# First four layer-norm tiles in one chain, last four normalised later, last output chunks in even shares

## The chip, the core and the metric

The kernel runs on one core of a Trainium2 chip. The metric is the device time of one execution in microseconds (us); the time before is the median of three executions. A profile shows one execution: what each engine does (TensorE, written PE, with its weight loads PEld; VectorE, DVE; ScalarE, ACT; GpSimd, POOL; SyncE, SP, which here only issues DMAs), when, and what ended the idle time before it. "L612" is line 612 of the kernel before.

## The reference

A transformer block's two branches over the same layer norm, x being 2048 tokens of 512 features:

```python
x = A_x
xn = _layernorm(x, axis=-1)
s = _A_ref(xn, A_wqkv, A_wo)                               # softmax attention, 32 heads of 16
g = _silu(_B_ref(xn, B_w_gate, B_w_up, B_w_down))          # ((xn Wg) * (xn Wu)) Wd, 1792 wide
return x + s * g
```

In `_A_ref`, `scores = einsum("bhqd,bhkd->bhqk", q, k) * scale`, then softmax, then the product with v, then `@ wo`. All is float32.

## The kernel before

Tokens are cut into 16 tiles of 128 and 4 chunks of 512. Matmuls read a float32 number as two parts, a rounded high part and the low rest, and make three products (high by high, high by low, low by high) for one. So each operand is *split*: a copy that rounds (`hi`), and a subtraction (`lo`).

**The start** (`early`, from L705). x is loaded tile by tile into `raw_x` (the buffer `ks` in the profile) and V, after the first four tiles the first weights of k, q (`w1r`, `w0r`) and of v. The layer norm of a tile is `ln_stats` (L204, L205, VectorE), the root `ln_root` (L208, ScalarE), five small operations `ln_scale` (L214 to L220) and `ln_apply` (L234 on VectorE for odd tiles below 8, L235 on ScalarE for the others). `ln_turn` (L246) transposes the tile on TensorE into a PSUM bank `xT`; for chunk 0 ScalarE copies it as the high part (L254) into `fh`, and `ln_low` (L259, VectorE) makes the low part `fl`. For the other chunks ScalarE copies it twice (L250, L251) and GpSimd subtracts. Tiles 0 and 1 go through that as a first chain, tiles 2 and 3 as a second, with matmuls of zeros (`warm`, L730) before and between them. `split_raw` splits the first weights on GpSimd; its first operation is made to wait for the last `ln_apply` of the four.

Then TensorE runs through 253 products (L267) of k, q and v, counted by `n`. A table `at` says which layer-norm step of tiles 4 to 15 is issued ahead of which product: for each chunk the products at which its four tiles' statistics, applications and transpositions stand. Every engine works in the order in which the program issues (a manual schedule; SP's order alone is the scheduler's). Some of the products make scores ahead (L610), whose row maxima VectorE takes (L612). q and k go through DRAM on the way to the scores (`KD`, `QD`).

**The main part.** 256 steps of the outer loop; in each, about 8 exponentials (`expo`: TensorE L632, ScalarE L634), 16 products pv with V (`block`, L645), and as many other products as a `Filler` gives: projections, the feed-forward branch, at last the output projection (`ending`). pv's result is added to a running sum: copied by ScalarE and added by GpSimd (L656, L63), and in the last rounds added by VectorE straight from PSUM (L653).

**The end.** `ending` goes through the output chunks in pairs of tiles: chunks 0 and 1 in two pairs each, the first pair of chunk 3, two pairs of chunk 2, the second pair of chunk 3. How many rounds a pair is spread over is an iterator in the outer loop:

```python
if fil.done:
    parts = iter([3, 2, 3, 2, 2, 2, 1, 2])
    fil = Filler(ending(), lambda n: next(parts))
```

For each chunk the finished heads, written to `OD` in DRAM by `finish`, are read back and split by `o_split` through `split_rows` (GpSimd). When a pair's product is done, `end` multiplies it on VectorE by the gate (L477), and `add` adds x on GpSimd and stores the result. The last heads are divided and transposed by `last_heads` (L692 to L697), after which the last products (L554) and multiplications follow.

Of the kernel before, what the change touches and what calls it, by code (L numbers as in the profile page):

```python
# [14 lines left out]
OP = mybir.AluOpType  # L15
# [6 lines left out]
NT = S // P  # L22
NC = S // 512
ND = D // P
# [7 lines left out]
LEAD = 86  # L32
# [16 lines left out]
def body(ctx, tc, x, wqkv, wo, wg, wu, wd, out):  # L49
    nc = tc.nc  # L50
# [72 lines left out]
    def soon(n, fn):  # L123

        if n:
            waiting.append((steps[0] + n, fn))
            waiting.sort(key=lambda w: w[0])
        else:
            fn()
# [45 lines left out]

    def split_raw(name, raw, after=None):
        hi, lo = [wtile(name + n) for n in "hl"]
        cast = pool.tensor_copy(hi, raw)
        if after is not None:
            tc.add_manual_dep(cast.ins, after.ins.name, BEHIND, reason="keeps the port free for the layer norm")  # L180
        pool.tensor_tensor(lo, raw, hi, op=OP.subtract)
        return hi, lo

    norm = {}
# [8 lines left out]
    def ln_open(tts):  # L193
        n = len(tts)
        g = [qp.tile([P, n, 2], F32, name=f"mv{n}", bufs=2)] + [qp.tile([P, n], F32, name=f"{v}{n}", bufs=2)
                                                              for v in ("r0", "e1", "mr")]
        for t, tt in enumerate(tts):
            norm[tt] = g, t
        norm[tts] = g
# [7 lines left out]
    def ln_root(tts):  # L207
        nc.scalar.activation(norm[tts][1], norm[tts][0][:, :, 1], AF.Sqrt, bias=eps)  # L208
# [25 lines left out]
            return nc.vector.tensor_scalar(xt, xt, e[:, t:t + 1], mr[:, t:t + 1], op0=OP.mult, op1=OP.add)  # L234
        return nc.scalar.activation(xt, xt, AF.Identity, bias=mr[:, t:t + 1], scale=e[:, t:t + 1])  # L235

    def split_rows(raw, hi, lo):
        pool.tensor_copy(hi, raw)
        pool.tensor_tensor(lo, raw, hi, op=OP.subtract)

    def ln_turn(tt):
        c, t = divmod(tt, 4)
        xt = tokens(tt)
        norm["x", tt] = pt = psum("x" if c else "s", f"xT{tt}")
        for d in range(ND):
            nc.tensor.transpose(pt[:, d * P:(d + 1) * P], xt[:, d * P:(d + 1) * P], ident)  # L246
        hi, lo = [x[c][:, :, t * P:(t + 1) * P] for x in (xh, xl)]
        if c:
            raw = norm["raws"][t]
            nc.scalar.activation(raw, pt, AF.Copy)  # L250
            nc.scalar.activation(hi, pt.rearrange("p (d q) -> p d q", d=ND), AF.Copy)  # L251
            pool.tensor_tensor(lo, raw.rearrange("p (d q) -> p d q", d=ND), hi, op=OP.subtract)
        else:
            nc.scalar.activation(hi, pt.rearrange("p (d q) -> p d q", d=ND), AF.Copy)  # L254

# [183 lines left out]
    def o_split(c, tiles):  # L439

        for d, (oh, ol) in enumerate(tiles):
            heads = 8 if c < NC - 1 or d < ND - 1 else 4
            n = heads * DH
            raw = (wtile(("w1r", "w0r")[d]).rearrange("p d q -> p (d q)") if d < 2 else
                   fst["fp"].tile([P, D], F32, name="wdr", bufs=2))
            dma(raw[:n], OD[c][8 * d:8 * d + heads, 0:DH])
            soon(4 + 5 * d // 2, lambda raw=raw[:n], oh=oh[:n], ol=ol[:n]: split_rows(raw, oh, ol))
        ops[c] = now[0], tiles

    def small_tiles():  # L450
# [31 lines left out]
        dma(out[tt * P:(tt + 1) * P], yt)  # L482

    def add(tt, yt, xt):
        pool.tensor_tensor(yt, yt, xt, op=OP.add)
        dma(out[tt * P:(tt + 1) * P], yt)

    def o_terms(c, t):
# [148 lines left out]
    def block(todo):  # L637

        i = todo[0][0]
        g = i // NC  # L640
        o = psum("st", f"pv{i}")
        for n, (_, kt, es) in enumerate(todo):
            for j in range(4):
                h0 = (4 * g + j) * VW
                nc.tensor.matmul(o[32 * j:32 * j + 32], V[:, kt, h0:h0 + 32], es[j],  # L645
                                 start=n == 0, stop=n == len(todo) - 1)
        if todo[-1][1] == NT - 1 and i == NU - 1:
            last_heads(o)
        elif todo[0][1] == 0:
            sums[i] = keep.tile([P, 512], F32, name="acc", bufs=2)  # L650
            nc.scalar.activation(sums[i], o, AF.Copy)
        elif now[0] > NU * NT - LEAD // 4:
            nc.vector.tensor_tensor(sums[i], o, sums[i], op=OP.add)  # L653
        else:
            part = part_tile()
            nc.scalar.activation(part, o, AF.Copy)  # L656
            pool.tensor_tensor(sums[i], sums[i], part, op=OP.add)
# [49 lines left out]
    def early():  # L707
# [22 lines left out]
                nc.tensor.matmul(psum("x", "warm"), idle[:, 0:P], idle, start=True, stop=True)  # L730

        warm(4)
        first = (0, 1), (2, 3)
        for tts in first:
            ln_open(tts)
        ln_stats(0)
        ln_stats(1)
        ln_root(first[0])
        ln_scale(first[0])
        ln_apply(0)  # L740
        ln_apply(1)
        ln_stats(2)
        ln_stats(3)
        ln_turn(0)
        ln_turn(1)
        warm(3)
        ln_root(first[1])
        ln_scale(first[1])
        ln_apply(2)
        last = ln_apply(3)  # L750
        ln_low(0)
        ln_low(1)
        ln_turn(3)
        ln_turn(2)
        ln_low(3)
        ln_low(2)
        wk, wq = [split_raw(f"w{which}", raw, last) for which, raw in zip((1, 0), wraw)]
        wv = [[etile().bitcast(F32R) for _ in range(ND)] for _ in range(2)]
        for d in range(ND):
            nc.scalar.activation(wv[0][d], raws[d], AF.Copy)  # L760
# [14 lines left out]
        at = {n: [] for n in range(253)}  # L775
        for c, stats, apply, turns in ((1, (0, 2, 4, 6), (26, 26, 26, 26), (38, 42, 46, 50)),
                                       (2, (16, 20, 26, 27), (60, 60, 62, 62), (70, 74, 79, 83)),
                                       (3, (30, 34, 36, 38), (73, 73, 85, 85), (100, 106, 112, 118))):
            for t in range(4):
                for n, fn in ((stats[t], ln_stats), (apply[t], ln_apply), (turns[t], ln_turn)):  # L780
                    at[n].append((fn, 4 * c + t))
# [158 lines left out]
    with tc.manual_schedule(engines=ORDERED):  # L940
# [4 lines left out]
        q = 0  # L945
        for b in range(NU * NT // 2):
            if fil.done:
                parts = iter([3, 2, 3, 2, 2, 2, 1, 2])
                fil = Filler(ending(), lambda n: next(parts))
            work = fil.begin()  # L950
            if b >= NU * NT // 2 - 2:
                last = TOTAL - 4 * (NU * NT // 2 - 1 - b)
            else:
                fits = min(9, max(7, int(2.6 + 0.62 * work))) if q + LEAD < TOTAL and work else 8
                need = 8 * (b + 1)
                last = min(max(q + fits, need + AHEAD[0]), need + AHEAD[-1], TOTAL - 4) if b else need + AHEAD[-1]
            count = last - q
            fil.spread(max(2, count - 2))
            for k in range(count):
                if k == count - 1:  # L960
                    run_all(gates)
                position(q)
                q += 1
                if 0 < k < count - 1 or count < 3:
                    fil.part()
            if b < NU * NT // 2 - 1:
                values([ready.pop(2 * b), ready.pop(2 * b + 1)])
# [34 lines left out]
```

## Time and profile before

| | us |
|---|---|
| median of three executions | 1711.33 |
| the three | 1711.22, 1711.33, 1714.48 |
| the profiled execution, its own time | 1711.65 |
| its span, first to last instruction | 1709.9 |
| TensorE busy in it | 1700.0 (99%) |
| VectorE, ScalarE, GpSimd busy | 1430.8, 1308.5, 888.2 |

A row of the timeline has start, duration, engine, line, operation, output<-input, shapes, how many were merged (x2), and in brackets how long the engine stood idle before it and what ended that. A row of the waits has the engine and line that waited, what it waited for, the total in us, how often, and the longest. A row of a window table has the stretch, its length, each engine's busy time and instructions (PE, PEld, DVE, ACT, POOL), the granted TensorE clock, the DMA share and GB/s. A row of the groups has the count, the busy time and the mean in ns, then the idle time before. SPq are the DMA issues of SyncE: the duration is that of issuing, not of the transfer.

### The profile page before, as it was taken

How to read it: one execution, taken by the hardware profiler on the slowest of the kernel's cores; microseconds unless marked ns; L12 is line 12 of the kernel's file. 1: busy time of each engine (PE TensorE's matmuls, PEld its weight loads, DVE VectorE, ACT ScalarE, POOL GpSimd, SP SyncE). 2: the span in 40 equal slices, each digit the busy share in tenths (PEclk: the TensorE clock that was granted, in tenths of full speed). 3: DMA queues.
4: the chain of work that ended last, by engine and by line, in shares of the span. 5: the costliest groups of instructions: out<-in, count | busy, mean ns of one | idle time of the engine just before them, and what ended most of it. 6: DMA issues, size and time to landing. Idle time of an engine off the chain costs nothing. (4 is left out here: it accounts for less than half of the span.)

```text
span 1709.9 us, 35015 instructions
## 1 busy us (share of the span) xinstructions
PE 1700.0 (99%) x13574; PEld 1043.2 (61%) x13574; DVE 1430.8 (84%) x2479; ACT 1308.5 (77%) x2568; POOL 888.2 (52%) x889
## 2 busy tenths in 40 slices
PE   9999999999999999999999999999999999999998
PEld 6666656666666666656656666666666666666655
DVE  6888888888888888888888888888888888888933
ACT  6357877777777778778877887877778787777774
POOL 5315545762644647446354672663637546346672
PEclk9999999999999999999999999999999999999999
DMA  5317623620241312412115220320225112011352
GB/s 209 108 48 215 242 105 126 152 66 20 63 91 36 103 57 67 90 48 61 30 53 133 71 70 21 94 70 27 62 83 121 54 36 73 27 54 48 124 177 78
DMA packets 117378, 145.79 MB, mean 85 GB/s; under 512 B 12636, under 2 KB 74332, under 8 KB 114524
## 3 DMA queue, kind: packets, MB, share of 16 engines
q1 hardware_dynamic: 117212, 143.55, 28.8%
q8 instruction: 107, 1.75, 0.4%
q14 instruction: 59, 0.48, 0.1%
HBM read 95.94 MB, written 47.45 MB: 84 GB/s over the span
## 5 line engine op out<-in xcount | busy, mean ns | idle before, releaser
L612 DVE TENSOR_REDUCE mx<-s 128x1 f32<-128x512 f32 x2048 | 1255.6, 683 | 210.5 <-PE s L610 172.6
L634 ACT ACTIVATE e<-t 128x512 f32<-128x512 f32 x2048 | 1100.9, 601 | 97.7 <-PE pv L645 46.6
L632 PE MATMUL t<-qs,ks 50*128 50x512 f32 x2048 | 781.9, 408 | 0.0
L610 PE MATMUL s<-ks,qs 48*128 48x512 f32 x2048 | 767.0, 409 | 0.2
L63 POOL TENSOR_TENSOR acc<-acc,part 128x512 f32<-128x512 f32 x214 | 279.8, 1308 | 582.5 <-ACT part L656 582.0
L632 PEld LDWEIGHTS t<-qs,ks 50*128 50x128 f32 x2048 | 359.2, 185 | 271.0 <-issue 110.2
L645 PE MATMUL pv<-e,V 128*32 128x512 f32 x4096 | 492.5, 598 | 0.0
L610 PEld LDWEIGHTS s<-ks,qs 48*128 48x128 f32 x2048 | 350.8, 185 | 26.5 <-issue 3.6
L656 ACT ACTIVATE part<-pv 128x512 f32<-128x512 f32 x214 | 128.1, 599 | 204.9 <-PE pv L645 204.9
L645 PEld LDWEIGHTS pv<-e,V 128*32 128x32 f32 x4096 | 107.0, 109 | 242.0 <-issue 216.8
L290 PE MATMUL g<-fh,w1h 64*128 64x512 f32 x224 | 90.5, 404 | 0.0
L286 PE MATMUL u<-fh,w0h 64*128 64x512 f32 x224 | 90.4, 404 | 0.0
L290 PE MATMUL y<-dh,hh 64*128 64x512 f32 x224 | 89.6, 400 | 0.0
L286 PE MATMUL y<-dh,hh 64*128 64x512 f32 x224 | 88.8, 397 | 0.0
L290 PE MATMUL u<-fh,w0l 64*128 64x512 f32 x224 | 88.2, 394 | 0.0
L290 PE MATMUL g<-fl,w1h 64*128 64x512 f32 x224 | 88.0, 393 | 0.0
L286 PE MATMUL g<-fl,w1h 64*128 64x512 f32 x224 | 88.0, 393 | 0.0
L286 PE MATMUL u<-fh,w0l 64*128 64x512 f32 x224 | 88.0, 393 | 0.0
L290 PE MATMUL g<-fh,w1l 64*128 64x512 f32 x224 | 88.0, 393 | 0.0
L286 PE MATMUL g<-fh,w1h 64*128 64x512 f32 x224 | 87.9, 392 | 0.0
L290 PE MATMUL u<-fl,w0h 64*128 64x512 f32 x224 | 87.8, 392 | 0.0
L286 PE MATMUL y<-dl,hh 64*128 64x512 f32 x224 | 87.8, 392 | 0.0
(262 smaller groups left out, 2982.5 us busy)
## 6 DMA issues: line engine op xcount, KB each, us to landing
w1r<-in_wg_dram SPq DMA_DIRECT2D x56, 256.0 KB
w0r<-in_wu_dram SPq DMA_DIRECT2D x56, 256.0 KB
wdr<-in_wd_dram SPq DMA_DIRECT2D x56, 256.0 KB
qs<-QD SPq DMA_DIRECT2D x64, 192.0 KB
ks<-KD SPq DMA_DIRECT2D x12, 768.0 KB
KD<-hl SPq DMA_DIRECT2D x16, 512.0 KB
QD<-hl SPq DMA_DIRECT2D x16, 512.0 KB
OD<-acc SPq DMA_DIRECT2D x31, 256.0 KB
```

What stands on the lines that cost most here:

```text
L63: got = getattr(self.engine, name)(*args, **kw)
L286: nc.tensor.matmul(outs[k], l[LOWER], r[LOWER], start=k == 0 and n == 0, stop=(stop or k == 0) and n == len(low) - 1, skip_group_check=k == 1)
L290: nc.tensor.matmul(outs[1 - k], l[UPPER], r[UPPER], start=k == 0 and m == 0, stop=(stop or k == 0) and m == len(high) - 1, skip_group_chec ...
L610: nc.tensor.matmul(o, QS[i][b:b + KB, pr, t * P:(t + 1) * P], k[b:b + KB, pr, kc * 512:(kc + 1) * 512], start=True, stop=True)
L612: nc.vector.tensor_reduce(MX[i][:, j, t, kc:kc + 1], o, axis=AX.X, op=OP.max)
L632: nc.tensor.matmul(o, k[b:b + KR, pr, kt * P:(kt + 1) * P], QS[i][b:b + KR, pr], start=True, stop=True)
L634: nc.scalar.activation(e, o, AF.Exp, scale=DH ** -0.5)
L645: nc.tensor.matmul(o[32 * j:32 * j + 32], V[:, kt, h0:h0 + 32], es[j], start=n == 0, stop=n == len(todo) - 1)
L656: nc.scalar.activation(part, o, AF.Copy)
```

## The change

Four things are changed.

1. The four tiles of chunk 0 go through the layer norm as one chain: four statistics, one root, one set of small operations (four wide), then the applications. The copies of the odd tiles' high parts go to VectorE, those of the even ones stay on ScalarE. The second group of warm-up matmuls is one instead of three and stands after the transpositions. In `split_raw` no longer the rounding waits, but the subtraction, and for the application of tile 1 instead of the last.
2. The applications of tiles 12 to 15 stand at products 87, 87, 93, 93 instead of 73, 73, 85, 85.
3. The rounds of the output pairs are 3, 2, 2, 2, 2, 2, 2, 2 instead of 3, 2, 3, 2, 2, 2, 1, 2. Their sum is the same.
4. In the last rounds (`late()`, the condition that the addition of pv's result had already), every second split of `o_split` and the additions in `add` are VectorE's, not GpSimd's.

```diff
     def split_raw(name, raw, after=None):
         hi, lo = [wtile(name + n) for n in "hl"]
-        cast = pool.tensor_copy(hi, raw)
+        pool.tensor_copy(hi, raw)
+        low = pool.tensor_tensor(lo, raw, hi, op=OP.subtract)
         if after is not None:
-            tc.add_manual_dep(cast.ins, after.ins.name, BEHIND, reason="keeps the port free for the layer norm")
-        pool.tensor_tensor(lo, raw, hi, op=OP.subtract)
+            tc.add_manual_dep(low.ins, after.ins.name, BEHIND, reason="keeps the port free for the layer norm")
...
-    def split_rows(raw, hi, lo):
-        pool.tensor_copy(hi, raw)
-        pool.tensor_tensor(lo, raw, hi, op=OP.subtract)
+    def split_rows(raw, hi, lo, on=None):
+        on = on or pool
+        on.tensor_copy(hi, raw)
+        on.tensor_tensor(lo, raw, hi, op=OP.subtract)
+
+    def late():
+        return now[0] > NU * NT - LEAD // 4
...
+        elif t % 2:
+            nc.vector.tensor_copy(hi, pt.rearrange("p (d q) -> p d q", d=ND))
         else:
             nc.scalar.activation(hi, pt.rearrange("p (d q) -> p d q", d=ND), AF.Copy)
...
-            soon(4 + 5 * d // 2, lambda raw=raw[:n], oh=oh[:n], ol=ol[:n]: split_rows(raw, oh, ol))
+            soon(4 + 5 * d // 2, lambda d=d, raw=raw[:n], oh=oh[:n], ol=ol[:n]:
+                 split_rows(raw, oh, ol, nc.vector if late() and d % 2 else pool))
...
     def add(tt, yt, xt):
-        pool.tensor_tensor(yt, yt, xt, op=OP.add)
+        (nc.vector if late() else pool).tensor_tensor(yt, yt, xt, op=OP.add)
...
-        first = (0, 1), (2, 3)
-        for tts in first:
-            ln_open(tts)
-        ln_stats(0)
-        ln_stats(1)
-        ln_root(first[0])
-        ln_scale(first[0])
-        ln_apply(0)
-        ln_apply(1)
-        ln_stats(2)
-        ln_stats(3)
-        ln_turn(0)
-        ln_turn(1)
-        warm(3)
-        ln_root(first[1])
-        ln_scale(first[1])
-        ln_apply(2)
-        last = ln_apply(3)
-        ln_low(0)
-        ln_low(1)
-        ln_turn(3)
-        ln_turn(2)
-        ln_low(3)
-        ln_low(2)
-        wk, wq = [split_raw(f"w{which}", raw, last) for which, raw in zip((1, 0), wraw)]
+        first = (0, 1, 2, 3)
+        ln_open(first)
+        for tt in first:
+            ln_stats(tt)
+        ln_root(first)
+        ln_scale(first)
+        port = ln_apply(1)
+        for tt in (0, 3, 2):
+            ln_apply(tt)
+        for tt in (1, 0, 3, 2):
+            ln_turn(tt)
+        warm(1)
+        for tt in (1, 3, 0, 2):
+            ln_low(tt)
+        wk, wq = [split_raw(f"w{which}", raw, port) for which, raw in zip((1, 0), wraw)]
...
-                                       (3, (30, 34, 36, 38), (73, 73, 85, 85), (100, 106, 112, 118))):
+                                       (3, (30, 34, 36, 38), (87, 87, 93, 93), (100, 106, 112, 118))):
...
-                parts = iter([3, 2, 3, 2, 2, 2, 1, 2])
+                parts = iter([3, 2, 2, 2, 2, 2, 2, 2])
```

What the change moves shows in the order of the instructions. First VectorE at the start, between the statistics of the first tiles and those of tile 4. Before (the second chain; `ks` holds the tiles, `r`, `e`, `mr` the small numbers of the norm, `xT` the transposed tile, `fh` and `fl` its parts):

```order
L214 RECIPROCAL r_206<-r_206 128x2
L217 SCALAR_TENSOR_TENSOR e_207<-r_206 128x2
L218 SCALAR_TENSOR_TENSOR e_207<-mv_205,e_207 128x2
L219 SCALAR_TENSOR_TENSOR e_207<-e_207,r_206 128x2
L220 SCALAR_TENSOR_TENSOR mr_208<-mv_205,e_207 128x2
L234 TENSOR_SCALAR ks_135<-ks_135,e_207,mr_208 128x512
L259 TENSOR_TENSOR fl<-xT_229,fh 128x4x128
L259 TENSOR_TENSOR fl<-xT_235,fh 128x4x128
L259 TENSOR_TENSOR fl<-xT_257,fh 128x4x128
L259 TENSOR_TENSOR fl<-xT_263,fh 128x4x128
```

And now (the only chain):

```order
L214 RECIPROCAL r_202<-r_202 128x4
L217 SCALAR_TENSOR_TENSOR e_203<-r_202 128x4
L218 SCALAR_TENSOR_TENSOR e_203<-mv_201,e_203 128x4
L219 SCALAR_TENSOR_TENSOR e_203<-e_203,r_202 128x4
L220 SCALAR_TENSOR_TENSOR mr_204<-mv_201,e_203 128x4
L234 TENSOR_SCALAR ks_135<-ks_135,e_203,mr_204 128x512 x2
L258 CAST fh<-xT_227 128x4x128
L258 CAST fh<-xT_239 128x4x128
L265 TENSOR_TENSOR fl<-xT_227,fh 128x4x128
L265 TENSOR_TENSOR fl<-xT_239,fh 128x4x128
L265 TENSOR_TENSOR fl<-xT_233,fh 128x4x128
L265 TENSOR_TENSOR fl<-xT_245,fh 128x4x128
```

Two casts have come in ahead of the four low parts, and all six now read tiles of the same chain.

Second, ScalarE between the first half of k and q of chunk 1 (`p_0_1`) and the first product of v behind it. Before (`V` holds tokens of tiles 8 to 15 until v overwrites them, `e` and `part` are raw copies, `xh_153` the high parts of chunk 2):

```order
L310 ACTIVATE qr<-p_0_1_476 128x512
L235 ACTIVATE V<-V,mr_340,e_339 128x512 x2
L250 ACTIVATE e<-xT_525 128x512
L251 ACTIVATE xh_153<-xT_525 128x4x128
L250 ACTIVATE e<-xT_550 128x512
L251 ACTIVATE xh_153<-xT_550 128x4x128
L250 ACTIVATE part<-xT_562 128x512
L251 ACTIVATE xh_153<-xT_562 128x4x128
L307 ACTIVATE hl<-p_0_1_520 128x512
L310 ACTIVATE qr<-p_0_1_520 128x512
L235 ACTIVATE V<-V,mr_340,e_339 128x512 x2
L351 ACTIVATE V<-v_594 128x32x16
```

And now:

```order
L316 ACTIVATE qr<-p_0_1_462 128x512
L254 ACTIVATE e<-xT_509 128x512
L255 ACTIVATE xh_153<-xT_509 128x4x128
L254 ACTIVATE e<-xT_534 128x512
L255 ACTIVATE xh_153<-xT_534 128x4x128
L254 ACTIVATE part<-xT_546 128x512
L255 ACTIVATE xh_153<-xT_546 128x4x128
L313 ACTIVATE hl<-p_0_1_506 128x512
L316 ACTIVATE qr<-p_0_1_506 128x512
L235 ACTIVATE V<-V,mr_326,e_325 128x512 x4
L357 ACTIVATE V<-v_578 128x32x16
```

The pair of applications that stood ahead of the copies of `xT_525` now stands with the other pair, behind all of them.

Third, VectorE in the last rounds, from the second pair of chunk 1 (`dl` takes its tiles) to the second pv of the last group of heads. Before:

```order
L677 STREAM_TRANSPOSE acc<-tr 128x512
L477 TENSOR_TENSOR dl<-z_2_25314,dl 128x512
L477 TENSOR_TENSOR dl<-z_3_25315,dl 128x512
L653 TENSOR_TENSOR acc<-pv_25444,acc 128x512
L653 TENSOR_TENSOR acc<-pv_25526,acc 128x512
```

And now (`w0r` and `wdr` hold heads of chunk 2 read back from `OD`, `hl` and `dh` their parts):

```order
L684 STREAM_TRANSPOSE acc<-tr 128x512
L484 TENSOR_TENSOR dl<-z_2_25251,dl 128x512
L484 TENSOR_TENSOR dl<-z_3_25252,dl 128x512
L492 TENSOR_TENSOR dl<-dl 128x512 x2
L239 CAST hl<-w0r 128x512
L240 TENSOR_TENSOR dh<-w0r,hl 128x512
L660 TENSOR_TENSOR acc<-pv_25470,acc 128x512
L239 CAST hl<-wdr 128x512
L240 TENSOR_TENSOR dh<-wdr,hl 128x512
L660 TENSOR_TENSOR acc<-pv_25537,acc 128x512
```

Two additions and two splits have come in, one of the splits ahead of the next pv's addition and one behind it.

On TensorE the products of the output pairs fall into the rounds otherwise: chunk 1's first pair of tiles has 12 and 12 pairs of products in two rounds, where it had 8, 7 and 9 in three, and chunk 2's last has 12 and 12, where it had 24 in one.

2 lines of the change are left out of this document (1 added, 1 removed).

## The prediction

> **What bounds the kernel now.** I read the page's busy shares first, then the waits of TensorE over the first 80 us, then the timeline of the two places that the change touches.
>
> ```profile
> span 1709.9 us, 35015 instructions
> PE 1700.0 (99%) x13574; PEld 1043.2 (61%) x13574; DVE 1430.8 (84%) x2479; ACT 1308.5 (77%) x2568; POOL 888.2 (52%) x889
> PE xT L246 <- ACT xh L251: 1.2, 1, 1.2
> ```
>
> TensorE is busy 99% of the span, so nothing that only shortens another engine counts. What can be won is time in which TensorE stands, or streams thinly: the start, one 1.2 us wait behind ScalarE, and the last rounds.
>
> **Part 1, the first four tiles.** A single chain needs the statistics of all four tiles, so it starts when the last tile has landed. SP's queue rows tell when: it issues the next x loads as earlier ones land.
>
> ```profile
> SPq L63 <- DMA ks<-in_x_dram: 0.6, 2, 0.4
> 6.72 1.07 SPq L63 DMA_DIRECT2D ks<-in_x_dram  x2
> 3.50 0.69 DVE L204 BATCH_NORM_STATS2 st<-ks 128x6 f32<-128x512 f32 x1 [2.11 <-DMA ks<-in_x_dram]
> 4.33 0.66 DVE L204 BATCH_NORM_STATS2 st<-ks 128x6 f32<-128x512 f32 x1
> 5.24 0.30 ACT L208 ACTIVATE r<-mv,eps 128x2 f32<-128x2 f32 x1 [3.02 <-DVE mv L205]
> 6.56 0.81 ACT L235 ACTIVATE ks<-ks,mr,e 128x512 f32<-128x512 f32 x1 [1.02 <-DVE mr L220]
> 10.99 0.55 DVE L234 TENSOR_SCALAR ks<-ks,e,mr 128x512 f32<-128x512 f32 x1
> 12.28 1.09 ACT L254 ACTIVATE fh<-xT 128x512 fp32r<-128x512 f32 x2 [0.48 <-PE xT L246]
> 13.51 0.70 PE L267 MATMUL p<-fh,w1h 128*128 128x512 f32 x2 [0.83 <-ACT fh L254]
> 12.91 1.29 DVE L259 TENSOR_TENSOR fl<-xT,fh 128x512 fp32r<-128x512 f32 x2 [0.18 <-ACT fh L254]
> 14.11 0.68 DVE L204 BATCH_NORM_STATS2 st<-ks 128x6 f32<-128x512 f32 x1
> L326 DVE COPY qr<-p 128x512 f32<-128x512 f32 x13 | 8.9, 681 | 0.0
> ```
>
> Tiles 0 and 1 are there at 3.50 and by 4.33; the next two landings release SP at about 6.02 and 6.72, so these are tiles 2 and 3. One tile's statistics take 0.8 us (3.50 to 4.33). In the new chain tile 2's start at 6.02, tile 3's at 6.83, and the root follows at about 7.75, not at 5.24. Root to scaling takes 1.32 us (5.24 to 6.56), so the scalings start at 9.06. The first scaled tile is ready at 9.61 (0.55 us), its copy out of PSUM starts 0.74 us later (11.54 to 12.28), at 10.35, and the others follow half a microsecond apart, as ScalarE's two do in 1.09 us. VectorE's copies of tiles 1 and 3 cost 0.68 us each (its copy from PSUM above, the nearest row) and end at about 12.05; ScalarE's of 0 and 2 end at 12.5. The products start 0.14 us after the last copy (13.37 to 13.51): 12.65 instead of 13.51, 0.86 us earlier. The four low parts follow on VectorE at 0.6 us each, 12.05 to 14.4, and hand over to the statistics of tiles 4 to 7 at 14.4 instead of 14.11: **0.3 us later**. Before, VectorE did two of the four low parts under the second chain; now all four, and two copies, come after it.
>
> ```profile
> 19.87 0.69 DVE L313 TENSOR_TENSOR hl<-p,hl 128x512 fp32r<-128x512 f32 x1 [0.28 <-ACT hl L307]
> 21.46 1.52 ACT L235 ACTIVATE ks<-ks,mr,e 128x512 f32<-128x512 f32 x2 [1.63 <-DVE mr L220]
> 22.34 0.20 PEld L246 LDWEIGHTS xT<-ident,ks 128*128 128x128 f32 x2 [0.30 <-ACT ks L235]
> 27.13 0.79 SPq L63 DMA_DIRECT2D qs<-QD  x2
> 30.78 0.73 PE L610 MATMUL s<-ks,qs 48*128 48x512 f32 x4
> 33.84 0.30 PEld L267 LDWEIGHTS p<-xh,w0h 128*128 128x128 f32 x2 [0.50 <-ACT V L351]
> ```
>
> Who takes the 0.86 us? TensorE already waits at 22.34 for the scaling of tile 4, and that is VectorE's queue: statistics, low part of k, two more statistics, low part of q at 19.87, root and scale. The 0.3 us go into the 0.28 us that VectorE waited there, so the scaling stays at 21.46 and TensorE waits 1.1 us instead of 0.3. The store of k leaves with k's low part, 0.3 us later, and the way through DRAM ends in the load of 27.13 that the first score (30.78) reads; that may cost 0.3 us, which the waits at 33.84 (0.50) take up. GpSimd's split of k's weights hangs on the first scaling now and ends at about 11, before it is needed; the two warm-up matmuls that go (four rows at 0.46 us) leave time in which TensorE waits anyway. I put part 1 at **0**, between -0.9 (all of it) and +0.6 (twice the slip).
>
> The second scaling on VectorE runs while GpSimd may start w1l (1.3 us). The Trainium skill (SBUF — State Buffer, SBUF: two separate sides) says that the two share one port pair, held by whoever comes first for a whole instruction. No row before shows such a meeting; if GpSimd came first, the sum would be 1.3 us worse, but its release comes from the end of the first scaling, and the second starts before that.
>
> **Part 2, tiles 12 to 15 normalised later.** Two scalings leave ScalarE's queue at 37.01 and stand behind the next pair of copies.
>
> ```profile
> 31.79 1.52 ACT L235 ACTIVATE V<-V,mr,e 128x512 f32<-128x512 f32 x2 [3.21 <-POOL mr L63]
> 37.01 1.53 ACT L235 ACTIVATE V<-V,mr,e 128x512 f32<-128x512 f32 x2
> 38.90 0.61 ACT L251 ACTIVATE xh<-xT 128x512 fp32r<-128x512 f32 x1
> 37.54 0.86 PE L267 MATMUL p<-xl,w0h 128*128 128x512 f32 x3
> 39.56 0.66 PE L246 MATMUL xT<-ident,V 128*128 128x128 f32 x4 [1.17 <-ACT xh L251]
> 42.11 0.79 SPq L63 DMA_DIRECT2D ks<-KD  x2
> 47.19 0.73 PE L610 MATMUL s<-ks,qs 48*128 48x512 f32 x4
> 44.99 0.60 ACT L351 ACTIVATE V<-v 128x512 f32<-128x512 f32 x1 [1.15 <-PE v L267]
> ```
>
> ScalarE works without a pause from 31.79 to 43.84 (1.15 us before 44.99), and the copy that frees the bank for the fourth transposition ends at 39.51; TensorE waits 1.17 us for it. Without the scalings (1.53 us, of which the next copy overlaps 0.1) it ends at 38.1, before TensorE comes. Then the four scalings run in a row, about 41.1 to 44.1, where ScalarE had those 1.15 us to spare; the copy of V slips 0.25 us, and another bank covers it. **-1.2 us**, between 0 and -1.3. What is late next is the key load of 42.11, which does not move: by the 3.6 us from 27.13 to 30.78 it is there at about 45.8, and the scores that need it come at 46.0 instead of 47.19.
>
> **Part 3, the last rounds.** A round is eight exponentials, sixteen pv products and a share of the output products. Before, the first two tiles of chunk 1 get 3 rounds (8, 7 and 9 pairs of products) and the last two of chunk 2 get 1 (24); now each gets 2 of 12. The windows run from one round's pv products to another's: the three thin rounds, two even ones, the fat one.
>
> ```profile
> 1628.91:1645.61 16.70, 16.61 (x122) 8.40 (x121) 3.43 (x9) 13.51 (x28) 14.69 (x15) 1.00 0.50 163
> 1669.46:1681.39 11.93, 11.93 (x98) 6.73 (x97) 1.38 (x2) 8.75 (x18) 0.13 (x1) 1.00 0.00 0
> 1681.39:1690.47 9.08, 9.06 (x74) 5.84 (x73) 2.05 (x4) 4.83 (x10) 2.53 (x2) 1.00 0.34 115
> PEld t L632 <- ACT e L634: 10.4, 17, 0.8
> ```
>
> An even round takes 5.97 us and the fat one 9.08, so a pair costs (9.08-5.97)/12 = 0.26 us; three thin rounds with 24 pairs instead of 36 should take 3 x 5.97 - 12 x 0.26 = 14.8 us, and take 16.70, because TensorE waits there for exponentials (10.4 us in 17 waits over the tail). Four rounds before: 16.70+9.08 = 25.78; after: 4 x 5.97 = 23.88, so -1.9. The first two now also carry ScalarE's part copy and tanh; for that I take off 0.1: **-1.8**, between 0 and -1.9.
>
> VectorE gets eight adds and four splits from GpSimd. Its row says 0.69 us for a like form (GpSimd's 1.29 bounds it from above), and it has idle time before each pv copy:
>
> ```profile
> 1636.62 0.69 DVE L653 TENSOR_TENSOR acc<-pv,acc 128x512 f32<-128x512 f32 x1 [5.58 <-PE pv L645]
> 1697.81 0.42 DVE L692 TENSOR_TENSOR acc<-pv,acc 128x256 f32<-128x256 f32 x1 [4.65 <-PE pv L645]
> 1650.67 0.37 SPq L63 DMA_DIRECT2D OD<-acc  x1
> 1654.46 0.60 SPq L63 DMA_DIRECT2D wdr<-OD  x1
> L63 POOL TENSOR_TENSOR hh<-hh 128x512 f32<-128x512 f32 x6 | 7.6, 1288 | 13.9 <-DVE hh L477 13.9
> ```
>
> At most four added operations (2.8 us) stand between two pv copies, under 4.65 us or more of idleness: price 0; uncovered, they would cost their 2.8 us a round. The last split waits for OD's way through DRAM (store 1650.67, load 1654.46, by the same difference there at 1658), and pv's copy behind it comes 8 us later (1628.9 plus six even rounds and its own pv products): covered. On SP's queue that store now stands behind two loads into hh, which wait for hh's outputs to land; those outputs leave a round, 6 us, earlier than before.
>
> **Sum:** 0 - 1.2 - 1.8 = -3.0 us against the profiled 1711.65 us (span 1709.9 and 1.75 around it). The median, 1711.33, lies 0.32 lower, so I forecast 1711.3 - 3.0 = **1708.3 us**.
>
> **Rivals.**
> A, the start keeps its 0.86 us. VectorE's chain would have to end that much sooner, with shorter copies than 0.68 us; for it speaks that TensorE's products do start earlier, against it the wait at 22.34. -3.9: 1707.4.
> B, a wait comes back: the key load holds the scores at 47.19, or ScalarE's extra work stretches the even rounds. Slack there is 0.2 us and little more. -1.2 instead of -3.0: 1710.1.
> C, the array goes slow again. The first eight warm-up matmuls took 0.85 us each, the later six 0.46:
>
> ```profile
> 1.45 6.78 PE L730 MATMUL warm<-acc 128*128 128x512 f32 x8 [1.45 <-DVE acc L91]
> 8.94 2.74 PE L730 MATMUL warm<-acc 128*128 128x512 f32 x6
> ```
>
> Now TensorE stands from 8.2 to 9.65 and the second group shrinks to one. If half pace lasted the 6.8 us of that first group again, it would cost 3.4 us, less the 1.1 us of wait at 22.34: -3.0 + 2.3 = -0.7, 1710.6. The Trainium skill (TensorE: Matmul & The Clock Gate, What's actually happening) has the clock halved only after an idle window of 3.4 us; by that rule it stays fast, and the trace, where a full stop of 1.17 us at 39.56 is followed by matmuls at the usual pace, agrees.
> D, slower: VectorE's queue in the tail. Every added operation meets GpSimd and waits one of its 1.29 us operations out; then four take 8 us, more than the 4.65 to 5.58 us of idleness, and pv's copy, whose bank TensorE needs again two products later, comes late. At 1.3 us in seven rounds, +9.1 - 3.0 = +6.1: 1717.4. Against it: in most rounds GpSimd has lost the very work that VectorE got.
>
> **How the numbers follow.** About 0.2% (3.4 us) is what a measurement of this kernel can tell from no change, and the forecast lies just inside. Forecast 0.52 (of it 0.20 beyond 0.2%, 0.32 within), A 0.14, B 0.16, C 0.07, D 0.11. Faster 0.20+0.14 = 0.34; within 0.32+0.16+0.07 = 0.55; slower 0.11. The range goes from all lower bounds (-0.9-1.3-1.9 = -4.1: 1707.2), less 0.8 for the spread of runs and rounds, to C at its worst and a little of D: 1706.4 to 1712.2.
>
> **What would show it.** Right: products from about 12.65, yet the transposition of tile 4 still at 22.3; no ScalarE wait before the transposition at 38.3; ten equal rounds of 5.97 us before the last. Wrong: transposition of tile 4 before 22 (A), scores after 46 waiting (B), products at half their pace after 12.65 (C), VectorE without idle time before its pv copies (D).

## The result, and the profile after

| | before | after |
|---|---|---|
| median of 15 executions each, same chip (us) | 1713.03 | 1709.15 |
| lowest and highest | 1710.98, 1714.63 | 1708.35, 1712.11 |
| span of the profiled execution | 1709.9 | 1707.0 |

The ratio is 0.9978, 95% interval 0.9971 to 0.9985: 2.6 to 5.0 us less. The spans of the profiled executions differ by 2.9 us, and 3.0 were forecast; the medians differ by 3.9. (By their own times, 1711.65 and 1709.17, the profiled executions differ by 2.5: outside the span one has 1.8 us and the other 2.2.) So there are two questions: whether the 2.9 us are made of the forecast terms, and where the other microsecond is. The interval holds 3.0 too, so the medians alone do not prove that there is such a microsecond; the spread of the runs, below, says more.

The page of the kernel after, span and busy times:

```profile
span 1707.0 us, 34993 instructions
PE 1695.4 (99%) x13570; PEld 1042.1 (61%) x13570; DVE 1441.9 (84%) x2492; ACT 1307.8 (77%) x2565; POOL 872.2 (51%) x873
```

The waits of TensorE in it (engine, line, what it waited for: total us, times, longest):

```profile
PE xT L250 <- DVE ks L234: 2.7, 1, 2.7
PE xT L250 <- ACT ks L235: 0.5, 1, 0.5
PE s L617 <- DMA ks<-KD: 0.4, 1, 0.4
PE s L617 <- DMA qs<-QD: 0.3, 1, 0.3
```

The 1.2 us behind ScalarE's copy are gone. The 2.7 us stand ahead of the first transposition, where warm-ups ran before; the three short waits are new. The timeline of the kernel after shows where (start, duration, engine, line, and in brackets the idle time before):

```profile
12.33 1.16 PE L273 MATMUL p<-fh,w1h 128*128 128x512 f32 x4
22.01 0.66 PE L250 MATMUL xT<-ident,ks 128*128 128x128 f32 x4 [0.47 <-ACT ks L235]
31.29 0.71 PE L617 MATMUL s<-ks,qs 48*128 48x512 f32 x3 [0.26 <-DMA qs<-QD]
35.10 0.73 PE L617 MATMUL s<-ks,qs 48*128 48x512 f32 x4
38.17 0.60 PE L250 MATMUL xT<-ident,V 128*128 128x128 f32 x4
45.81 0.46 PE L617 MATMUL s<-ks,qs 48*128 48x512 f32 x1
46.71 0.70 PE L617 MATMUL s<-ks,qs 48*128 48x512 f32 x3 [0.43 <-DMA ks<-KD]
38.49 0.81 SPq L63 DMA_DIRECT2D KD<-hl  x2
42.48 0.79 SPq L63 DMA_DIRECT2D ks<-KD  x2
43.50 0.81 SPq L63 DMA_DIRECT2D QD<-hl  x2
```

Read against before's rows, event by event (s_n is the nth group of four scores from 0, us after minus before):

| event | after | minus before |
|---|---|---|
| first product | 12.33 | -1.18 |
| transposition of tile 4 | 22.01 | -0.33 |
| s_1 | 35.10 | -0.07 |
| s_2, behind the place of part 2's wait | 38.92 | -1.47 |
| s_4 begins; it meets the key load | 45.81 | -1.38 |
| s_5 | 50.50 | -0.52 |
| first pv product | 105.80 | -0.51 |
| pv at the head of the three once thin rounds | 1628.01 | -0.91 |
| pv behind them | 1645.94 | +0.33 |
| pv behind the once fat round | 1687.63 | -2.84 |
| end | 1707.0 | -2.90 |

Part 1 gives its lead back before s_1, part 2 wins 1.4 and loses 0.9 at the key load, and part 3 wins 1.93 between the last rows. The 0.4 between 105 and 1628 us answers to no step of the change and lies within the scatter of profiles: from the first pv product to the end, the nine with the even rounds took 1601.2 to 1601.8 us. The windows of the kernel after answer to those of before (stretch, length, busy time and instructions of PE, PEld, DVE, ACT, POOL, clock, DMA share, GB/s):

```profile
1628.01:1645.94 17.93, 17.93 (x146) 10.13 (x145) 8.12 (x16) 14.28 (x28) 12.14 (x12) 1.00 0.49 143
1681.67:1687.63 5.96, 5.96 (x51) 3.33 (x49) 0.69 (x1) 4.41 (x10) 0.00 (x0) 1.00 0.57 176
```

The three thin rounds of 16.70 us are now three even ones of 17.93, the fat one of 9.08 is 5.96, and the ten rounds last 5.86 to 6.04.

### The profile page after: what moved, and what is told of

Its sections match the earlier page's. It is cut to its first block, busy times and chain, and to the rows that moved or that the text cites. A ratio compares the mean times of both kernels' runs of the same rounds, so it can differ in the third digit from the quotient of the medians.

```text
span 1707.0 us, 34993 instructions
## 1 busy us (share of the span) xinstructions
PE 1695.4 (99%) x13570; PEld 1042.1 (61%) x13570; DVE 1441.9 (84%) x2492; ACT 1307.8 (77%) x2565; POOL 872.2 (51%) x873
## 3 DMA queue, kind: packets, MB, share of 16 engines
q8 instruction: 107, 1.75, 0.4%
## 4 chain that ended last, share of the span: by engine, by line
PE 96%; DVE 1%; DMA 1%; issue 0%; POOL 0%; ACT 0%; SPq 0%; POOLq 0%
PE pv L652 28%; PE t L639 19%; PE s L617 12%; PE g L292 6%; PE g L296 5%; PE y L292 5%; PE y L296 5%; PE u L292 5%; PE u L296 4%; PE p L292 3%; PE v L273 2%; PE p L296 2%; PE z L292 2%; PE z L296 1%; DVE mx L619 0%
```

## The experiments

Twelve kernels, in four sets; each set was timed beside its own runs of before (medians 1712.36, 1712.96, 1713.40, 1712.40).

| | median (us) | ratio to before, 95% interval | span of the profile |
|---|---|---|---|
| e1 part 1 alone | 1712.63 | 1.0001, 0.9992 to 1.001 | 1712.5 |
| e2 part 2 alone | 1710.06 | 0.9984, 0.9975 to 0.9993 | 1708.1 |
| e3 part 3 alone | 1710.62 | 0.9991, 0.9983 to 1.0 | 1708.9 |
| e4 parts 3 and 4 | 1711.19 | 0.9991, 0.9982 to 1.0 | 1709.3 |
| e5 before, later scores | 1711.81 | 0.9993, 0.9984 to 1.0002 | 1709.8 |
| e6 after, later scores | 1708.50 | 0.9972, 0.9961 to 0.9983 | 1706.8 |
| e7 after, q first | 1708.28 | 0.9974, 0.9964 to 0.9984 | 1706.6 |
| e8 after, all splits on VectorE | 1708.81 | 0.9981, 0.9972 to 0.9989 | 1706.9 |
| e9 e6 and e7 together | 1707.97 | 0.997, 0.9958 to 0.9981 | 1705.3 |
| e10 e9 without part 1 | 1708.39 | 0.9971, 0.9961 to 0.9982 | 1706.8 |
| e11 after, q's store of chunk 1 later | 1715.66 | 1.0013, 1.0004 to 1.0022 | 1713.8 |
| e12 before, code shifted | 1711.42 | 0.9997, 0.9988 to 1.0006 | 1709.6 |

### The parts one by one: e1 to e4

e1 is before with the change's hunks in `split_raw` and `ln_turn` and the one from `first = ...` on. The others:

```diff
e2  -(73, 73, 85, 85)   +(87, 87, 93, 93)
e3  -iter([3, 2, 3, 2, 2, 2, 1, 2])   +iter([3, 2, 2, 2, 2, 2, 2, 2])
e4  e3, with `late`, `split_rows(..., on)`, `o_split` and `add` of the change
```

> The kernel before with part 1 alone (one chain for the first four tiles, copies by VectorE and ScalarE, one late warm-up matmul, the moved wait of GpSimd's split). Theory: the products start near 12.3 us as in the changed kernel, but what they win is taken back in front of the first scores, whose q comes through DRAM and SP's queue; the scores s_1 (35.17 in before) come within 0.15 us of that, and the span changes by -0.1 (-0.3 to +0.3). Rival A: the start keeps its 0.9 to 1.2 us; s_1 comes at about 34.1 and the span is 0.9 or more shorter. Rival: four low parts and two copies on VectorE cost the statistics behind them; s_1 later than 35.3.

> The kernel before with part 2 alone (scalings of tiles 12 to 15 at products 87, 87, 93, 93). Theory: the 1.17 us wait at 39.56 goes, the scores s_2 come at about 39.0 instead of 40.39 (-1.4), but the scores behind them meet the key load that comes at 46.0 to 46.7; from 51 us on some 0.5 us are left, span -0.5 (-0.3 to -0.9). Rival: the key load's lateness in the changed kernel belongs to its shifted start and not to this part; then the whole 1.2 to 1.4 us stay, span -1.3. Rival: the bank of tile 11 is not what held; then s_2 stays at 40.4 and nothing changes.

> The kernel before with part 3 alone (output pairs over 3, 2, 2, 2, 2, 2, 2, 2 rounds; the additions of x and the second splits stay on GpSimd). Theory: the rounds alone carry the gain; ten even rounds of 5.97 us, span -1.9 (-1.7 to -2.1). Rival: the even rounds need the work taken off GpSimd (its splits and additions come later than the products that read them); then TensorE waits for a split of chunk 2 or 3 and the gain is under 1 us or a loss. Rival: a position of the thin rounds matters and not their number; then rounds of another length than 5.97.

> The kernel before with parts 3 and 4 (even rounds, and in the last rounds additions of x and every second split on VectorE). Theory: VectorE's added work costs and brings nothing on the path before the last scores; the span equals that of part 3 alone within 0.2 us, so about -1.9 to -2.0 against before. Rival: part 4 itself brings 0.3 or more (GpSimd frees SP's queue and the splits), then this one is shorter than part 3 alone. Rival D in small: VectorE's copies of pv come late and rounds are longer than 5.97.

**Part 1.** e1's span was 2.6 us longer than before, which none of its theories had; that came at 60 us, below. Its s_1 came at 34.80, not within 0.15 of 35.17: a single start is a poor measure, since the first product came at 12.83 to 13.51 in six profiles with the same old start (before, e2, e3, e4, e5, e12). Over profiles: with the old start the first product came at 13.09 in the mean and tile 4's transposition at 21.94; with the one chain (after, e1, e6, e8, e11) at 12.28 and at 21.96. So 0.8 us are won and all given back by tile 4. Rival A falls.

**Part 2.** e2's s_2 came at 38.75 (39.0 expected), s_5 lost 0.6 of it; from s_1 to the first pv product it took 70.37, before 71.14: -0.8. Its span, 1.7 shorter, was outside the expected 0.3 to 0.9; 0.7 of that lies in the main part. Its median is 2.3 under before's, though, and its 11 runs lie between 1709.73 and 1710.39, where the 33 of before went from 1710.32 to 1714.65.

**Parts 3 and 4.** From the head of the thin rounds to the pv behind the fat one, e3 was 1.88 shorter than before and e4 1.89. Part 3 carries the gain, part 4 nothing. The windows of e3, then of e4, over the three rounds and the once fat one:

```profile
1629.82:1647.77 17.95, 17.95 (x146) 10.20 (x144) 4.61 (x10) 14.28 (x28) 16.39 (x17) 1.00 0.49 156
1683.55:1689.50 5.95, 5.95 (x50) 3.32 (x49) 0.69 (x1) 4.39 (x10) 0.00 (x0) 1.00 0.54 176
1630.32:1648.27 17.95, 17.95 (x147) 10.44 (x145) 8.12 (x16) 14.27 (x28) 12.19 (x12) 1.00 0.48 144
1684.03:1689.99 5.96, 5.96 (x51) 3.33 (x49) 0.69 (x1) 4.41 (x10) 0.00 (x0) 1.00 0.55 176
```

Their spans are only 0.98 and 0.54 shorter, for the same reason as e1's:

### One packet of code behind a store

SP's queue around the keys of chunk 2 and TensorE at the scores that need them, in before:

```profile
52.85 0.81 SPq L63 DMA_DIRECT2D KD<-hl  x2
56.16 0.79 SPq L63 DMA_DIRECT2D ks<-KD  x2
60.12 0.96 PE L610 MATMUL s<-ks,qs 48*128 48x512 f32 x6
61.58 2.01 PE L267 MATMUL v<-e,xh 128*128 128x512 f32 x8
```

The same in e1, with two windows of e1 there:

```profile
52.17 0.81 SPq L63 DMA_DIRECT2D KD<-hl  x2
57.45 0.79 SPq L63 DMA_DIRECT2D ks<-KD  x2
```

```profile
60.56 0.46 PE L612 MATMUL s<-ks,qs 48*128 48x512 f32 x1 [0.62 <-DMA ks<-KD]
61.42 0.71 PE L612 MATMUL s<-ks,qs 48*128 48x512 f32 x3 [0.39 <-DMA ks<-KD]
62.63 3.07 PE L269 MATMUL v<-e,xh 128*128 128x512 f32 x8
```

```profile
59.83:63.25 3.42, 2.41 (x11) 1.50 (x10) 3.21 (x6) 0.37 (x1) 0.00 (x0) 1.00 0.19 27
63.25:66.66 3.41, 3.41 (x9) 2.36 (x8) 0.56 (x1) 2.20 (x4) 1.29 (x1) 0.50 0.14 56
```

The load waits for the store to end. From store to load before took 3.31 us (52.85 to 56.16), here 5.28. Two scores then wait for the keys, and then the clock stands at 0.50 for 3.4 us, eight products taking 3.07 us instead of before's 2.01. The DMA view of e1 for 55.3 to 56.8 us shows what the engines moved at the store's end:

```profile
DMA packets 4, 0.02 MB, mean 14 GB/s; under 512 B 1, under 2 KB 1, under 8 KB 3
q8 instruction: 1, 0.02, 3.9%
q1 hardware_dynamic: 3, 0.00, 2.0%
```

The packets one by one, from the traces (start to end, bytes, queue):

```
before  the store's last data ends at 55.74                              load issued at 56.16
e1      55.36-56.29 16384 q8; 56.28-56.51 2048 q1; 56.50-56.72 2048 q1   load issued at 57.45
e3      55.73-56.66 16384 q8; 56.65-56.88 2048 q1                        load issued at 57.82
```

All of the store is done by then but one or two packets of 2 KB, and these start one after another as the 16 KB packet of the instruction queue ends. The trace does not name the DMA engine of a packet; that they share one is read from these times. In e4 it is the same (store to load 5.36), and in e6 and e9, introduced below, the packet lies at the head of the store's stream, and store to load took 4.69 and 4.89 us. Where it lies outside the stream, store to load took 3.3 to 3.5 us in eight profiles of nine (in e11 a load of q ran beside the store: 4.86). Over these scores TensorE lost 1.6 us in e3, 1.8 in e4, and 3.3 in e1 with the clock. The runs of before fall into three such groups: of the 26 of the second set, 6 lie from 1711.0 to 1711.6, 15 from 1712.5 to 1713.8, 5 from 1714.2 to 1714.8. The profile on which the forecast was built has no stretched store, and no profile of before itself from the two later groups is on record: that they are such stores is a reading from e1, e3 and e4, whose losses of 3.3 and of 1.6 to 1.8 us fit the steps between the groups. Two edits of before test whether this is what spreads them:

```diff
e5  -142 + 13 * n: 6 for n in range(8)   +151 + 12 * n: 6 for n in range(8)
e12 -warm(3)
    +warm(1)
    +for _ in range(8):
    +    nc.tensor.matmul(psum("x", "warm")[:, 0:8], idle[:, 0:P], idle[:, 0:8], start=True, stop=True)
```

> The kernel before, with the scores that first need the keys of chunk 2 issued 9 products later (2.1 us; their groups at products 151, 163, ... 235 instead of 142, 155, ... 233). In the profiles of parts 1, 3 and 4 alone the store of chunk 2's keys (issued at 52.2 to 52.7) took 5.3 us until the load behind it, in before and in part 2 alone 3.3; each time one packet of 16 KB of the instruction queue lay on one DMA engine for 0.93 us, with the store's last two packets behind it, and the scores then cost TensorE 1.65 us, or 3.3 where its clock also fell to 0.5 for 3.4 us. Theory: this is what spreads the runs of before over 4.3 us (1710.3 to 1714.65) and lifts their median; with the scores later the stretched store is covered, the runs lie within 1.5 us of each other and the median is 1.0 to 2.0 us under before's. Rival: the spread has another cause (the main part, the clock); it stays over 3 us and the median is the same. Rival: later scores press VectorE's row maxima against the end of the products; then some 0.5 us longer in every run.

> The kernel before, with two of the three warm-up matmuls of the second group replaced by eight narrow ones (128x8), still matmuls of zeros: TensorE's instruction stream is 24 instructions longer ahead of the first product, and nothing else changes. The instruction queue's 16 KB packets are TensorE's (107 of them are 1.75 MB, its 27,348 instructions at 64 bytes); the second of the run comes at 50.1 to 51.6 in the profiles whose store of chunk 2's keys takes 3.3 us, and at 55.4 to 56.0 in those where it takes 5.3. Theory: where that packet falls hangs on where a line of the code ends; with the stream longer the line ends some 12 matmuls, about 3 us, earlier, so that even when it is late the packet lies ahead of the store; the runs lie within 1.5 us and the median is 1.0 to 1.5 us under before's, as with the later scores. Rival: the packet is drawn by the scores' wait and not by the code's length, or the stretched store has another cause; then the runs still spread over 3 us or more and the median is that of before.

With the scores 2.1 us later, the 11 runs lay within 0.86 us (1711.28 to 1712.14) and the median 1.15 under before's, as expected; the whole interval of the ratio does not exclude no change, but 26 runs of before spread over 3.8 us. The profile of e5 has no stretched store, so it does not show one covered; those of e6 and e9, with the same later scores, do: 4.69 and 4.89 us from store to load, and no score waits. The third theory holds in part: from s_2 to the first pv product the four profiles with the later scores (e5, e6, e9, e10) took 66.20 to 66.30 us, before and e12 65.92 and 65.96. The later scores cost some 0.3 us themselves, and e5's runs begin 0.3 above the lowest of before.

With nothing but TensorE's code 24 instructions longer, the packet came at 47.7, and 9 of 11 runs lay between 1711.24 and 1711.7, the median 0.98 under before's. Two runs at 1713.3 and 1713.7 were not expected; no profile shows them. Since 7 of the 15 runs of before beside it also lay under 1711.9, e12 alone is weak evidence.

So the missing microsecond is, as far as the runs show it, this: the change, through part 2, takes most runs out of the two later groups. e2 had none of 11 there, while the runs of e3 and e4, without part 2, still spread over 4.9 and 3.8 us. Profiles with part 2 and the old place of the scores (after, e2, e7, e8, e11) have the packet at 50.1 to 51.4, ahead of the store, as before's has at 51.6; e1, e3 and e4 at 55.4 to 56.0. Why it is some 4 us late in one execution and not in another, and why part 2 keeps it early, stays open.

### What takes back part 2 and part 1: e6, e11, e7

```diff
e6  e5's edit, and  -104: 4, 113: 4, 124: 6   +108: 4, 117: 4, 129: 6
e11 (which, c) == (0, 1):  the low part and `qk_store` in at[101], `load_q(1)` behind it
e7  k(0): -load_k(0, [0])    q(0): +load_k(0, [0]) behind q's store
    -(2, (16, 20, 26, 27),   +(2, (26, 27, 28, 29),
```

> The changed kernel with the scores of chunk 1's keys 4 products later and those of chunk 2's 9 later. Theory: the key load of chunk 1 no longer holds the scores (0.43 us of waiting, and another 0.43 us lost because the first of the four scores runs alone), so all of part 2's 1.4 us stay: span about 1706.1 instead of 1707.0, median -0.9 to -1.2 against the changed kernel, so about -4.8 against before. Rival: what was lost there is not the key load but ScalarE's queue; then the span stays at 1707.0.

> The changed kernel, with the low part of q of chunk 1 on GpSimd, and with it q's store, put behind the low part of tile 12 (store issued at about 48.8 instead of 43.50). Theory: two things made the key load of chunk 1 late, each measured in the traces: the store of the keys ended later because one 8 KB packet of the instruction queue (0.31 us) lay in its tail (3.99 us from store to load instead of 3.30), and the load itself took 0.45 us longer (42.48 to 46.7, against 42.11 to 45.86 before) because q's store, 1.2 us earlier now, runs beside it. Here the second goes: the last of the four scores s_4 come at about 46.25 instead of 46.71, s_5 (50.50) some 0.4 to 0.8 us earlier. The first stays: store to load again 3.9 to 4.0. Rival: q's store does not matter; the scores stay at 46.7 and s_5 at 50.5 (against the time of s_1, to leave out the start).

> The changed kernel with q's store of chunk 0 ahead of the key load on SP's queue (before, it stood behind that load, which waits for the keys' store: ready at 20.2, issued at 22.28), and the statistics of tiles 8 to 11 moved behind the scaling of tiles 4 to 7 on VectorE. Theory: what takes back the start's 1.2 us is VectorE's queue ahead of tile 4 (0.47 us of waiting at 22.0) and q's way through DRAM ahead of the first scores (0.26 us, and as much lost because the first score runs alone); with both gone, the transposition of tile 4 comes at 21.5, the first four scores run together at about 30.1, s_1 at 34.4 instead of 35.10, and the span is 0.7 shorter (-0.4 to -0.9). Rival: something else holds there (ScalarE's copies, the tiles' loads); then s_1 stays at 35.1 and nothing is won.

**The key load.** In the change the keys' store of chunk 1 leaves 0.32 us earlier (38.49), and the load behind it 0.37 later (42.48 instead of 42.11). The DMA view of the kernel after for 41.2 to 42.0 us:

```profile
q1 hardware_dynamic: 28, 0.02, 9.9%
q14 instruction: 1, 0.01, 2.4%
```

An 8 KB packet of 0.31 us, from 41.26, stands ahead of this store's last three packets of 2 KB. Every kernel with part 2 has such a packet inside the store's stream: store to load took 3.95 to 4.00 us in all eight, and 3.30 or 3.31 in before, e1, e3, e4, e5 and e12, where it runs beside the last packets and none starts behind it. With e6 the four scores run together again (47.34), and s_1 to first pv took 70.08 us instead of 70.70: 0.6 of the 0.9 is back, and the other 0.3 is what the later scores cost by themselves (above). The span is only 0.14 shorter, since s_1 came 0.24 later and the main part took 0.24 longer.

e11 put q's store out of the load's way. s_1 to s_5 took 14.83 us instead of 15.40, as expected (0.4 to 0.8), and store to load stayed at 4.00. From the load to the scores that waited for it took 3.78 us, in the kernel after 4.23. So the second cause is shown by taking it away; the first is shown only by its packet, there in all eight and missing in the other six, as no run takes the packet out of part 2. The run itself missed: q's load now waited for q's store at the head of SP's queue (48.60 to 53.83), and the store of chunk 2's keys behind it left at 54.67 instead of 52.34. The waits of TensorE in e11:

```profile
PE s L624 <- DMA ks<-KD: 3.6, 2, 3.1
```

**The start.** With q's store ahead of the waiting key load, and four statistics moved back, first product to s_1 took 21.90 us in e7, 22.77 in after, 21.66 before. The four first scores run together (30.19), and tile 4 no longer waits. So those two, SP's order and VectorE's queue, took part 1's lead back: 0.87 us of the 1.11 by which after is slower here than before. e7 changes both and does not part them. The span is 0.34 shorter (0.4 to 0.9 was expected), with a first product that came 0.36 later.

### VectorE's queue: e8

```diff
-split_rows(raw, oh, ol, nc.vector if late() and d % 2 else pool))
+split_rows(raw, oh, ol, nc.vector if late() else pool))
```

> The changed kernel with all splits of the last rounds on VectorE instead of every second (up to six more pairs of a cast of 0.4 us and a subtraction of 0.7 to 1.0). Theory: VectorE's idle time before its pv additions (0.6 to 5.3 us in the changed kernel) takes most of it, even rounds stay at 5.97 us, span +0 to +0.3. Rival D: the additions of pv come late in the rounds with splits, TensorE waits for their banks; those rounds last over 6.5 us, span +1 or more.

VectorE's busy time in the three rounds rose from 8.12 to 12.60 us, and their length from 17.93 to 17.96. Rival D falls, and price 0 for part 4 holds with twice the splits. A window of e8 over these rounds:

```profile
1627.84:1645.80 17.96, 17.96 (x146) 10.61 (x144) 12.60 (x20) 14.26 (x28) 8.91 (x8) 1.00 0.61 190
```

And VectorE's timeline in e8 at two of pv's additions:

```profile
1635.85 0.69 DVE L660 TENSOR_TENSOR acc<-pv,acc 128x512 f32<-128x512 f32 x1 [1.72 <-PE pv L652]
1641.82 0.69 DVE L660 TENSOR_TENSOR acc<-pv,acc 128x512 f32<-128x512 f32 x1 [0.60 <-PE pv L652]
```

Ahead of the first, the idle time fell from 4.83 us in the kernel after to 1.72; ahead of the second it was 0.59 there already. pv itself still ends it in both, so neither addition is late.

### Both edits, with and without part 1: e9, e10

> The changed kernel with both earlier edits together: scores of chunks 1 and 2 later, and q's store first with the statistics of tiles 8 to 11 later. Theory: the two gains are in different places and add, 0.45 to 0.5 at the start and 0.4 to 0.6 at the scores; the first pv products come at about 104.9 (105.80 in the changed kernel), span about 1706.0 (1707.0), give or take the 0.25 us by which the main part differed from run to run; median about 5 us under before's. Rival: the start's gain is eaten by the scores that now wait for VectorE or for the keys; then the first pv products come at 105.3 as with either alone.

> The same as the kernel with both edits, but with the first four tiles in two chains as before (part 1 left out). It tells what part 1 is worth once what took it back is gone. Theory: products start at 13.4 instead of 12.4, and all behind is later by the 0.5 to 1.0 us, since nothing in between waits for anything else; span 0.5 to 1.0 longer than with part 1. Rival: the one chain is worth nothing even then (its six operations on VectorE come ahead of the statistics of tiles 4 to 7); then the transposition of tile 4 comes at 21.7 in both, and the spans agree within 0.2 us.

e9 is the fastest: first pv at 103.59, no wait of TensorE behind the first transposition, span 1705.3, median 5.4 us under before's. Beside e10 its profile is 1.6 us shorter, but that is luck in part: its first product came at 11.58, 0.7 ahead of the mean of the one chain. The spans of seven runs each have medians of 1705.8 and 1706.5, and the times of 1707.97 and 1708.39. With the takers gone part 1 looks worth some 0.4 to 0.7 us, which is not shown: the intervals overlap, and e9's runs spread more (2.2 us, e10's 0.5).

## Why the prediction was right, and where not

**Part 1, 0:** right, by the forecast's path. The products came at 12.33 (12.65 forecast) and the lead was gone at s_1. Details were off: the statistics of tile 4 slipped by 0.1 instead of 0.3 (14.20), so its scaling came at 21.15 and TensorE waited 0.47 instead of 1.1; and the queue that took back the rest was SP's, where q's store stood behind a load that waits (ready at 20.2, issued at 22.28); the forecast named only a slip of 0.3 on that way.

**Part 2, -1.2:** the mechanism was right and the wait went (-1.4 at s_2). The step that failed is "What is late next is the key load of 42.11, which does not move: ... it is there at about 45.8". It moved: issued at 42.48 and in use at 46.71, by a code packet in the store's tail (+0.7, read from the packets) and q's store, 1.2 us earlier, beside the load (+0.45, e11). Half a microsecond stayed. Rival B named the place, though not the cause, and its price, 1.8 lost, was twice the 0.9.

**Part 3, -1.8:** right in kind and near in size: -1.9, the upper bound, in the changed kernel and in e3 and e4 alike. The 0.1 taken off for ScalarE's copy and tanh was not needed. That exponentials hold the thin rounds fits the profiles: over the three rounds TensorE's weight loads waited for them nine times (3.7 us) before, and three times (2.5 us) in the kernel after and in e3. No run changes the exponentials alone.

**Part 4, 0:** right (e3 against e4, and e8). Its reason was read from two rows, though. The idle time was not 4.65 us or more everywhere: ahead of four of the nine whole pv additions before it was only 0.5 to 0.8. What held is that no pv addition came late.

**The sum:** -3.0 for a profile that changed by -2.9; 0.75 too much on part 2 is made up by 0.1 on part 3 and by 0.4 of drift in the main part and the start's remainder, so the sum was better than its terms, by luck. The time, 1708.3, was 0.85 under the median, and there too two errors met. The base was 1.7 too low: 1711.3 was the median of three runs, two of them in the lowest of three groups, and 15 runs gave 1713.03. The medians then fell by 0.9 more than forecast, for a reason that the forecast does not have: the spread.

**Rival C:** no half pace after the first chain: TensorE stood 2.70 us (by the forecast 8.2 to 9.65; its clock rose at 5.13 instead of 7.68, so the warm-ups ended earlier), and the products of 12.33 went at the usual pace. But the clock did fall elsewhere, for less (below).

## What to carry to other kernels

When a wait is removed ahead of a transfer through DRAM, price the store, the code packets and the other stores that will now run beside it, not only the engine's queue. A serial queue that waits for a store holds ready stores behind it (2.1 us in the kernel after): put these first, unless that makes another wait, as in e11. Before forecasting against a profile, look at the spread of the runs: here most of it seems to be a wait that the profiled execution happened not to have.

## What the hardware showed unexpectedly

**Code loading delays data.** The 16 KB instruction packets in the tails of the three stretched stores took 0.93 to 0.96 us, the 8 KB one in the kernel after 0.31. Measured from the store's issue, the store's last packet ended 1.7 us later in e1 than in before and 1.5 in e3, and 0.5 later behind the 8 KB packet; the load that waits was issued 2.0, 2.1 and 0.7 later. What makes up the difference stays open. The Trainium skill (Runtime: NRT & Kernel Launch, Instruction fetch mechanics) has the sequencer fetch its code over a DMA queue of its own in 16 KiB blocks, and calls the cost of crossing a block mostly hidden. The trace agrees on the 16 KB for TensorE (107 packets, 1.75 MB), and no wait in the list of TensorE's waits above is for code; what was not hidden is the delay of another queue's store.

**The clock fell without a long stop.** In e1 it stood at 0.5 from 63.25 to 66.66 (the rows above): behind a window of 3.4 us in which TensorE was busy for 2.41 us and waited for 0.62 and 0.39. At the start of the kernel after, TensorE stood for 2.70 us, and the clock stayed:

```profile
5.10:8.51 3.41, 1.86 (x5) 0.55 (x3) 2.15 (x8) 0.30 (x1) 0.61 (x1) 1.00 1.05 354
8.51:11.93 3.42, 2.27 (x18) 2.00 (x18) 2.77 (x8) 2.42 (x4) 2.18 (x3) 1.00 1.06 402
```

The Trainium skill (TensorE: Matmul & The Clock Gate, What's actually happening) has it fall after an idle window of some 3.4 us, the windows running free of the program. The length agrees: from its rise at 5.22 us to its fall at 63.25 e1's clock record has 58.03 us, 17 windows of 3.413. If idle means without matmuls, e1 contradicts it; and busy time alone is not the measure either, since 1.86 us kept the clock at the start. In e11 a window with 0.47 us busy, while TensorE waited 3.1 us for the keys, was followed by 6.83 us at 0.5. What the measure is stays open.

**VectorE and GpSimd held each other up, at no cost here.** In the kernel after, at 1653 to 1657 us (timeline):

```profile
1655.33 1.52 DVE L239 CAST hl<-w0r 128x512 fp32r<-128x512 f32 x1
1654.94 1.62 POOL L63 TENSOR_TENSOR dh<-w1r,hl 128x512 fp32r<-128x512 f32 x1
```

A cast of the same shape takes 0.43 us while GpSimd stands (1660.77), a subtraction of the same shape 1.28 beside VectorE's multiplications (1652.56): 1.1 and 0.3 us more where cast and subtraction run at the same time. pv's next addition (1659.81) still found VectorE idle, for 1.94 us.
